# Reordering the prologue of a fused attention and two-layer MoE kernel: seven first-layer chunks of batch 1 moved into the first script

## The chip, the cores and the metric

The kernel runs on one core of one Trainium2 chip. The metric is the device time of one execution in microseconds (us). Three runs of the kernel before gave 869.15, 870.41 and 870.77 us; the median is 870.41 us.

## The reference

```python
# attention: 4 batches, 8 heads, 576 positions, head size 64
scores = (1/8) * q @ k.T          # heads 0-3: window of 32; heads 4-7: window of 128, every 4th
attn = softmax(where(mask, scores, -1e9))
x = attn @ v                      # -> 2304 tokens x 512
# first block, d_ff = 1536
h = sigmoid(x @ w_gate) * (x @ w_val)
y = h @ w_out                     # 2304 x 512
# second block, d_ff = 2048
h2 = y @ w_in
out = (max(h2,0) + alpha*min(h2,0)) @ w_out2
```

All inputs and outputs are float32. q, k and w_gate are scaled up, so that the softmax and the sigmoid are sharp.

## The kernel before

Every large product is made from float16 halves: an operand is scaled by a power of two, its high half is a float16 copy and its low half is what the copy leaves. Three matmuls (high x high, high x low, low x high) then stand for one float32 product. So each weight goes through a **preparation**: a load (SP queue), a decode of three bit operations for each 512-column piece (VectorE, `decode`, L180, L184, L188), a bound (ScalarE, `bound`, L195), a power of two from it (a one-column matmul at L149, two small VectorE operations in `root_power`, one on GpSimd), and a split into high and low half. `split_weight` does the split either with two ScalarE copies and a GpSimd subtraction (L169), or, with its `on_dve` flag, with one ScalarE copy and one VectorE operation (L173).

The work goes batch by batch. A half-batch `hb` is one batch and one kind of head (0, 1 are batch 0; 2, 3 batch 1; 4 belongs to batch 2). For each there are scores (`qk_mm`, `qk_sub`), softmax (`exponent`, `p_sums`, `p_scale`), a transpose, and the product with v (`pv_mm`, `pv_x`), which leaves x in halves in `xh`.

The first layer has 12 **chunks** of 128 gate and 128 value columns. Chunk m of batch b is `gv_mm(b, m, "g")` and `gv_mm(b, m, "v")` (24 matmuls each, L582, also callable by halves of 12), then `gv_sigmoid` (ScalarE), `gv_multiply` (VectorE, L600, frees the value's PSUM pair) and `gv_halves` (a ScalarE copy, and a subtraction on GpSimd or VectorE, L169), which leaves the tile `gt[b, m]`. The second product of the block, `o1_mm(b, d, ...)` (L627, `d` = 0 to 3, quarters of 18 matmuls in the first script), reads all twelve `gt` tiles of its batch and the split `w_o`. `o1_y` takes it out of PSUM and stores it to `y_dram`. Three pairs of PSUM banks rotate over all g, v and o products.

The order of the prologue is written out by hand: the string `FIRST` is a list of tasks, run one after the other, and every engine and the SP queue execute their instructions in that order. Some task names: `lqk hb`, `lv hb`, `lgv m`, `lo d r` are loads of q and k, v, gate and value weights of chunk m, and a third of output weights d; `dec`, `spl` are decode and split of chunk m; `odec`, `orow`, `ospl` the same for the output weights, `opow` their power of two; `g`, `v`, `sig`, `mul`, `half` the parts of a chunk; `o`, `oy` those of the second product; `plo`, `pm` the low half and the scaling of the softmax; `prep n` some steps of the preparation of the second block's weights; `warm n` n matmuls on zeros. A last argument of 1 or 0 on `spl`, `ospl`, `plo`, `half` chooses VectorE or GpSimd.

In the kernel before, `FIRST` holds all of batch 0's first layer, its `o` products with three chunks of batch 1 behind and between the last of them, and the attention of half-batches 0 to 3 and the scores and softmax of 4. After it come loops: for batch 1 the chunks from `EARLY` on, then its `o`, then batches 2 and 3; the last batch overlaps the second block. `prepare(n)` gives out steps of the second block's preparation at two places of every chunk and three of every `o` product. Loaded words and v tiles share a pool `yp` of 8 buffers of 4 KB for each partition; the `gt` tiles of a batch share 12 buffers of a pool `gp`.

```python
for m in range(EARLY if b == 1 else 0, M1):
    gv_mm(b, m, "g")
    if m:
        gv_halves(b, m - 1, late)
    gv_sigmoid(b, m)
    prepare(3)
    gv_mm(b, m, "v")
    gv_multiply(b, m)
```

Of the kernel before, what the change touches and what calls it, by code (L numbers as in the profile page):

```python
# [1567 lines left out]
wsum 0; phi 1 0; pvx 0 1 0; plo 1 0 0; plo 1 2 0; wpow 0; pvm 1 0; pvx 0 1 1; dec 1; pvm 1 1 4; spl 0 0; pvx 1 1 1;
spl 0 1; g 0 0 0; pvx 1 0 0; pvx 1 0 1; lgv 4; wb 1; wsum 1; qkm 2 0; wpow 1; pvx 1 1 0; spl 1 0; wgs 0; g 0 0 1; dec
2; g 0 1 0; wgs 1; spl 1 1 1; lgv 5; dec 3; wb 2; v 0 0 0; wsum 2 0; sig 0 0; qkm 2 1; lgv 7; wpow 2; spl 2 0 1; spl 2  # L1570
1 1; v 0 0 1; wb 3; g 0 1 1; wgs 2; mul 0 0; wsum 3; wpow 3; spl 3 0; v 0 1 0; sig 0 1; v 0 1 1; lo 1 0; g 0 2 0; spl
3 1; v 0 2 0; g 0 2 1; dec 4; mul 0 1; qks 2 0; xb 2; xb 3; wb 4; qkm 2 2; sig 0 2; lo 0 0; xsum 1; half 0 1 1; wsum
4; v 0 2 1; dec 5; g 0 3 0; qks 2 1; wpow 4; wb 5; wsum 5 0; g 0 3 1; qks 2 2; spl 4 0; spl 4 1 1; half 0 0 1; wpow 5;
mul 0 2; exp 2; v 0 3 0; dec 6; wgs 3; sig 0 3; v 0 3 1; xpow 1; spl 5 0 1; lgv 8; wb 6; spl 5 1 1; g 0 4 0; wsum 6; v
0 4 0; wgs 4; half 0 2 1; mul 0 3; lgv 10; wpow 6; spl 6 0; g 0 4 1; sig 0 4; spl 6 1; dec 7; wgs 5; g 0 5 0; wb 7;
half 0 3; v 0 4 1; wsum 7; rs 2; g 0 5 1; lgv 9; sig 0 5; wpow 7; g 0 6 0; mul 0 4; wgs 7; spl 7 0; pm 2; v 0 5 0; dec
8; v 0 5 1; tr 2; spl 7 1; g 0 6 1; wb 8; wgs 6; v 0 6 0; wsum 8; half 0 4; wpow 8; dec 9; sig 0 6; vhi 2; g 0 7 0;
mul 0 5; lv 4; phi 2; v 0 6 1; spl 8 0; lqk 3; g 0 7 1; plo 2; spl 8 1 1; wb 9; sig 0 7; lgv 11; mul 0 6; vlo 2; half
0 6 1; half 0 5 1; g 0 8 0; wsum 9 0; lo 0 2; v 0 7 0; lo 0 1; wpow 9; g 0 8 1; dec 10; pvm 2 0; pvx 2 0 1; spl 9 0;
spl 9 1 1; wgs 8; v 0 7 1; wb 10; wsum 10; mul 0 7; v 0 8 0; pvx 2 0 0; wpow 10; sig 0 8; dec 11; spl 10 0 1; spl 10  # L1580
1; v 0 8 1; g 0 9 0; half 0 7 1; wb 11; pvm 2 1; wsum 11; g 0 9 1; pvx 2 1 0; v 0 9 0; odec 0 0 1 2; wpow 11; wgs 9;
orow 0 0 0; v 0 9 1; lo 2 0; orow 0 1 1; pvx 2 1 1; spl 11 0; orow 0 2 0; lo 2 2; qkm 3 0; lo 1 1; qks 3 0; spl 11 1
1; qkm 3 1; mul 0 8; wgs 10; g 0 10 0; xb 4; vhi 3; obd 0 1; obd 0 0; odec 1 0 1; lo 3 1; osum 0; half 0 8 1; qkm 3 2;
sig 0 9; opow 0; v 0 10 0; g 0 10 1; mul 0 9; v 0 11 0; vlo 3; half 0 9 0; wgs 11; v 0 10 1; lo 1 2; odec 1 2; ospl 0
0 1; qks 3 2; qks 3 1; lo 2 1; orow 1 2 0; sig 0 10; lo 3 2; orow 1 0 1; mul 0 10; orow 1 1 0; v 0 11 1; g 0 11 0; g 0
11 1; ospl 0 1; obd 1 0; lqk 4; obd 1 1; osum 1; o 0 0 0; exp 3; odec 2 0 1 2; opow 1; sig 0 11; orow 2 2 0; orow 2 1
1; mul 0 11; orow 2 0 1; o 0 0 1; rs 3; ospl 1 0 1; half 0 11 1; obd 2 1; obd 2 0; pm 3; osum 2; ospl 1 1; o 0 0 2;
# [89 lines left out]
```

## Time and profile before

| what | value |
|---|---|
| runs, us | 869.15, 870.41, 870.77 (median 870.41) |
| span of the profiled execution, first to last instruction | 870.0 us |
| TensorE busy, mean granted clock | 830.0 us (95%), 0.982 of full speed |
| VectorE, ScalarE, GpSimd busy | 618.3, 440.7, 286.7 us |
| DMA | 166.9 MB, mean 192 GB/s |
| the chain that ended last, by engine | PE 76%, DVE 13%, ACT 5%, DMA 4% |
| last matmul of `FIRST` ends (720th of L582) | 206.4 us |
| from 206.4 to 400 us | TensorE busy 193.6 of 193.6 us |

The profile shows one execution; its own time is the span, and what lies around the span is not recorded. The median of the runs is 0.4 us above it. PE is TensorE's matmuls, DVE VectorE, ACT ScalarE, POOL GpSimd, SP the queue that issues all transfers. A busy engine runs an instruction; "<-" after an idle time names what ended it. A granted clock of 1.00 is the upper of TensorE's two levels, 2.4 GHz; a mean between 0.5 and 1 says for how much of a stretch the lower, 1.2 GHz, was granted.

### The profile page before, as it was taken

The numbers are of one execution on the slowest core, as the hardware profiler recorded it, in microseconds if no ns is written. First come the engines' busy times: TensorE is split into PE (matmuls) and PEld (weight loads), VectorE is DVE, ScalarE is ACT, GpSimd is POOL, SyncE is SP. The second block draws the span as 40 slices with busy tenths as digits, with TensorE's granted clock in tenths as the row PEclk, the third lists the DMA queues.
The fourth block names the chain that finished last, engine by engine and source line by source line (L and its number), as shares of the span: only waits on it lengthen the run. The fifth ranks groups of instructions, "written<-read, shape, count | busy, mean of one in ns | idle before, by whom it ended". The sixth has DMA issues, their size and how long they took to land.

```text
span 870.0 us, 21031 instructions
## 1 busy us (share of the span) xinstructions
PE 830.0 (95%) x8994; PEld 686.7 (79%) x8994; DVE 618.3 (71%) x1031; ACT 440.7 (51%) x730; POOL 286.7 (33%) x261
## 2 busy tenths in 40 slices
...
GB/s 323 286 194 124 229 100 207 15 173 102 92 95 169 139 136 119 50 68 264 301 166 223 342 214 221 337 241 218 308 203 212 243 210 194 225 309 194 122 230 73
DMA packets 85181, 166.91 MB, mean 192 GB/s; under 512 B 5344, under 2 KB 57696, under 8 KB 85088
## 3 DMA queue, kind: packets, MB, share of 16 engines
...
## 4 chain that ended last, share of the span: by engine, by line
PE 76%; DVE 13%; ACT 5%; DMA 4%; issue 2%; POOL 1%; SPq 0%; ACTq 0%; DVEq 0%
PE banks L582 27%; PE banks L1204 18%; PE banks L959 17%; PE banks L627 11%; DVE plain L188 2%; DVE plain L184 2%; DVE plain L180 2%; PE banks L430 1%; PE banks L316 1%; DMA words<-w_out 1%; DMA words<-w_gate 1%; ACT junk L195 1%; DVE plain L199 1%; DMA w_i<-wi_dram 1%; DVE g_g L1045 1%
## 5 line engine op out<-in xcount | busy, mean ns | idle before, releaser
L582 PE MATMUL banks<-xh,w_gv 128*128 128x288 f16 x2304 | 295.5, 290 | 3.1 <-DVE gf L600 2.3
L582 PEld LDWEIGHTS <-w_gv 128*128 128x128 f16 x2304 | 226.1, 99 | 63.3 <-issue 3.2
L959 PE MATMUL banks<-yh,w_i 128*128 128x256 f16 x1536 | 187.1, 273 | 5.1 <-DMA w_i<-wi_dram 1.6
L959 PEld LDWEIGHTS <-w_i 128*128 128x128 f16 x1536 | 150.0, 98 | 24.0 <-issue 3.3
L627 PE MATMUL banks<-gt,w_o 128*128 128x288 f16 x1152 | 147.0, 288 | 0.3 <-POOL gt L169 0.2
L627 PEld LDWEIGHTS <-w_o 128*128 128x128 f16 x1152 | 112.0, 98 | 29.4 <-issue 0.4
L1204 PEld LDWEIGHTS <-g_gv 128*128 128x128 f16 x780 | 76.3, 98 | 8.8
L1204 PE MATMUL banks<-w,g_gv 128*128 128x256 f16 x612 | 75.5, 273 | 0.0
L997 ACT ACTIVATE neg<-banks 128x512 f32<-128x512 f32 x72 | 42.8, 594 | 57.2 <-DVE banks L1017 40.8
L1055 POOL TENSOR_TENSOR yh<-temp_y 128x512 f32<-128x512 f32 x16 | 26.5, 1659 | 125.7 <-DVE temp_y L1005 121.0
L600 DVE SCALAR_TENSOR_TENSOR gf<-banks,sg 128x576 f32<-128x576 f32 x48 | 36.0, 751 | 38.9 <-PE banks L582 27.3
L165 POOL TENSOR_SCALAR sc<-sc 128x1 f32<-128x1 f32 x35 | 11.4, 326 | 157.7 <-DVE sc L161 157.7
L1204 PEld LDWEIGHTS <-g_g 128*128 128x128 f16 x564 | 55.2, 98 | 6.4
L169 POOL TENSOR_TENSOR gt<-gf,gt 128x576 f16<-128x576 f32 x24 | 36.8, 1533 | 63.5 <-ACT gt L610 63.3
L195 ACT ACTIVATE junk<-plain 128x1024 bf16<-128x1024 f32 (+1 forms) x36 | 36.2, 1006 | 40.3 <-DVE plain L199 28.3
L595 ACT ACTIVATE sg<-banks,sc 128x576 f32<-128x576 f32 x48 | 35.3, 735 | 38.1 <-PE banks L582 27.7
L610 ACT ACTIVATE gt<-gf 128x576 f16<-128x576 f32 x48 | 32.3, 676 | 41.3 <-DVE gf L600 41.3
L188 DVE SCALAR_TENSOR_TENSOR plain<-words,plain 128x512 uint32<-128x512 uint32 x68 | 50.8, 767 | 1.2
L184 DVE SCALAR_TENSOR_TENSOR plain<-words,plain 128x512 uint32<-128x512 uint32 x68 | 50.2, 759 | 1.2
L1204 PE MATMUL banks<-w,g_g 128*128 128x256 f16 x396 | 48.3, 273 | 0.0
L1005 DVE SCALAR_TENSOR_TENSOR temp_w<-neg,sc,banks 128x256 f32<-128x256 f32 x64 | 27.8, 475 | 25.1 <-ACT neg L997 25.1
L1045 DVE SCALAR_TENSOR_TENSOR g_gv<-temp_w,sc,g_gv 128x256 f16<-128x256 f32 (+1 forms) x37 | 26.0, 711 | 27.6 <-ACT g_gv L1041 27.6
...
## 6 DMA issues: line engine op xcount, KB each, us to landing
...
```

The costliest lines, as they stand in the source:

```text
L169: engine.tensor_tensor(out=lo, in0=src, in1=hi, op=ALU.subtract)
L184: nc.vector.scalar_tensor_tensor(out=d, in0=hi, scalar=0xC0000000, in1=d, op0=ALU.bitwise_and, op1=ALU.bitwise_or)
L188: nc.vector.scalar_tensor_tensor(out=d, in0=lo, scalar=29, in1=d, op0=ALU.logical_shift_right, op1=ALU.bitwise_or)
L195: nc.scalar.activation(junk[:, :src.shape[1]], src, AF.Square, accum_out=dst)
L582: nc.tensor.matmul(ps[:, h, :], lhsT=a, rhs=x_[:, H2 * h:H2 * h + H2], start=(kk == 0 and i == 0), stop=(kk == KD - 1 and i == 2),)
L595: nc.scalar.activation(halves(sg), ps, AF.Sigmoid, scale=sgx[b][:, m:m + 1])
L600: nc.vector.scalar_tensor_tensor(out=halves(gf), in0=ps, scalar=2.0 ** -15, in1=halves(sg), op0=ALU.mult, op1=ALU.mult)
L627: nc.tensor.matmul(ps[:, h, :], lhsT=a, rhs=x_[:, H2 * h:H2 * h + H2], start=(m == 0 and z == 0), stop=(m == M1 - 1 and z == 2),)
L959: nc.tensor.matmul(o, lhsT=h, rhs=l, start=(new and v == 0 and q == 1), stop=(q == total_), skip_group_check=True,)
L997: nc.scalar.activation(t[:, :2 * n], src[:, :2 * n], AF.Relu, scale=-1.0)
L1045: nc.vector.scalar_tensor_tensor(out=h[:, 1], in0=x_, scalar=s_al, in1=h[:, 0], op0=ALU.mult, op1=ALU.subtract)
L1204: nc.tensor.matmul(ps[:, H4 * t:H4 * t + H4].rearrange("p (c f) -> p c f", c=2), lhsT=a, rhs=x_, start=(first and k == 0 and t == 0 and z ...
```

## The change

`EARLY` goes from 3 to 7, so seven chunks of batch 1 (0 to 6) are tasks of `FIRST`, and the loop of batch 1 begins with chunk 7. Their order there is 1, 0, 2, 4, 5, 3, 6, and all stand ahead of batch 0's first `o`. Their `gt` tiles cannot all stay on chip while batch 0's twelve are in use: a new tag holds two (`HELD`), and tiles 1, 0, 4, 3 and 2 are stored to a DRAM tensor `g_dram` (`gst`) and loaded back into `gp` (`gld`) after batch 0's last `o`. Tiles 5 and 6 stay. The third piece of each output weight is decoded into a buffer of its own (`po`) and no longer into one of `yp`, and the `y` tile of `o1_y` shares the buffers of the sigmoid in place of those of `gf`.

```diff
-    EARLY = 3
+    EARLY = 7
+    HELD = 2
...
-            plain["o", d, 1] = yp.tile([P, 4, P], F32, tag="y", name="plain")
+            plain["o", d, 1] = wp.tile([P, 4, P], F32, tag="po", name="po")
...
+    g_dram = dp.tile([EARLY - HELD, P, 2, S], F16, name="g_dram")
...
-        if b == 1 and m < EARLY - 1:
-            t = gt[b, m] = ap.tile([P, 2, S], F16, tag=f"g{m}", name="gt")
+        if b == 1 and m < EARLY:
+            t = gt[b, m] = ap.tile([P, 2, S], F16, tag="g", name="gt", bufs=HELD)
...
+    def g_store(m):
+        nc.sync.dma_start(out=g_dram[m], in_=gt.pop((1, m)))
+
+    def g_load(m):
+        t = gt[1, m] = gp.tile([P, 2, S], F16, tag="g", name="gt")
+        nc.sync.dma_start(out=t, in_=g_dram[m])
...
-        dst = tp.tile([P, S], F32, tag="gf", name="y")
+        dst = tp.tile([P, S], F32, tag="sg", name="y")
...
-        "wgs": lambda m: x_gate_scale(0, m, m + 1),
+        "wgs": lambda m, b=0, e=0: x_gate_scale(b, m, max(e, m + 1)),
...
-        "gs": lambda b: x_gate_scale(b, 0, M1),
...
-            for m in range(EARLY if b == 1 else 0, M1):
+            m0 = EARLY if b == 1 else 0
+            for m in range(m0, M1):
                 gv_mm(b, m, "g")
-                if m:
+                if m > m0:
                     gv_halves(b, m - 1, late)
...
 FIRST = """
-lqk 0 3; warm 6 2; warm 8 5; lqk 1 3; qkm 0 0; qks 0 0; qkm 0 1; exp 0 0; qks 0 1 1; qkm 0 2; lv 0; exp 0 1; lv 1; rs
+lgv 0; dec 0 0; dec 0 1; lqk 0 3; warm 6 2; wb 0; warm 8 5; qkm 0 0; qkm 0 1; wsum 0; qks 0 0; wpow 0; lqk 1 3; exp 0
...
```

The whole of `FIRST` is written in a new order. Counted over it, 31 more instructions run on VectorE (322 for 291) and 7 fewer on GpSimd (81 for 88): on VectorE are now 12 of the `half` subtractions (2 before), 16 of the weight splits (10), 5 of the `plo` (none), 4 of the `ospl` (5), 19 of the `mul` (15) and 20 instructions of `prep` (13). On GpSimd stand 6 fewer `spl`, 5 fewer `half` and 5 fewer `plo`, one more `ospl`, and small one-column operations. The matmuls on zeros are the same 28, and the loads of activation tables are the same 14 in the whole program.

The head of the SP queue, which issues all transfers (words are weight pieces, second is q and k of half-batch 1, vc is v). Before:

```order
L1303 DMA mask_sb_80<-mask 128x516
L246 DMA k_93<-kt 128x2x224
L247 DMA q_92<-qbd 128x2x384
L246 DMA second_117<-kt 128x2x224
L252 DMA vc_173<-vk 128x1152
L252 DMA vc_181<-vk 128x1152
L499 DMA words_213<-w_gate 128x4x256
L499 DMA words_215<-w_val 128x4x256
```

And now:

```order
L1313 DMA mask_sb_80<-mask 128x516
L500 DMA words_93<-w_gate 128x4x256
L500 DMA words_95<-w_val 128x4x256
L247 DMA k_105<-kt 128x2x224
L248 DMA q_104<-qbd 128x2x384
L247 DMA second_169<-kt 128x2x224
L500 DMA words_279<-w_gate 128x4x256
L500 DMA words_281<-w_val 128x4x256
L253 DMA vc_283<-vk 128x1152
```

The rows between that repeat these kinds are left out: q and k come in three pairs for each half-batch. The weights of chunk 0 moved from behind all of half-batches 0 and 1 to the very front, and those of chunk 1 ahead of v.

VectorE between the last split of the first layer's weights (w_gv) and the first decode of the output weights (words to plain). Now:

```order
L174 SCALAR_TENSOR_TENSOR w_gv_1590<-plain,sc,w_gv_1590 128x4x128
L400 STREAM_TRANSPOSE pt<-s 128x1152
L276 SCALAR_TENSOR_TENSOR vh<-vc,sc,vh 128x1152
L170 TENSOR_TENSOR s<-pt,s 128x1152
L170 TENSOR_TENSOR gt<-gf,gt 128x576
L602 SCALAR_TENSOR_TENSOR gf<-banks,sg 128x576
L174 SCALAR_TENSOR_TENSOR xh<-banks,xh 128x2x144 x2
L181 TENSOR_SCALAR plain<-words 128x512 x2
```

Rows that repeat an earlier kind are left out. In the kernel before, the first decode of output weights (9 instructions) stood ahead of chunk 11's last split, and half-batch 3's v came 17 rows behind that decode and its transpose 46 rows. They now come first, so that batch 1's x is complete before any output weight is decoded. The two rows at L170 are a `plo` and a `half` that GpSimd did before.

The SP queue where the five tiles are stored and loaded back. Now:

```order
L616 DMA g_dram_85<-gt_2366 128x1152
L533 DMA words_2570<-w_out 128x4x256
L533 DMA words_2574<-w_out 128x4x256
L247 DMA k_2626<-kt 128x2x608
L248 DMA q_2625<-qbd 128x2x1152
L616 DMA g_dram_85<-gt_2526 128x1152
L616 DMA g_dram_85<-gt_2682 128x1152
L533 DMA words_2801<-w_out 128x4x256
L616 DMA g_dram_85<-gt_2798 128x1152
L616 DMA g_dram_85<-gt_2596 128x1152
L620 DMA gt_3170<-g_dram_85 128x1152
```

Nothing of this was there before. The first store is that of tile 1; the second and third, of tiles 0 and 4, stand behind two loads of output weights and the load of q and k of half-batch 5, which waits for the last scores of half-batch 4. Between the last store and the first load back stand loads of the second block's weights and of v, and three `y` stores (left out).

## Rows read from the trace of the kernel before

**Rows 1.** Stretches: us, PE, PEld, DVE, ACT, POOL busy (instructions), clock, DMA share, GB/s.
```profile
0.00:40.00 40.00, 29.64 (x606) 20.50 (x608) 27.22 (x61) 22.38 (x65) 12.65 (x19) 0.87 0.97 331
40.00:122.40 82.40, 71.48 (x833) 54.50 (x829) 71.20 (x127) 54.38 (x86) 43.85 (x43) 0.92 0.49 160
122.40:169.20 46.80, 38.42 (x406) 28.93 (x403) 41.71 (x59) 26.80 (x43) 24.95 (x23) 0.93 0.36 123
169.20:206.40 37.20, 37.18 (x471) 29.94 (x471) 25.80 (x44) 20.10 (x29) 7.12 (x9) 1.00 0.43 148
0.00:206.40 206.40, 176.72 (x2306) 133.87 (x2307) 165.92 (x290) 123.66 (x220) 88.57 (x93) 0.93 0.54 182
...
400.00:600.00 200.00, 195.28 (x1903) 162.29 (x1902) 153.76 (x236) 108.08 (x187) 88.97 (x81) 1.00 0.70 245
600.00:870.00 270.00, 264.42 (x2420) 236.29 (x2417) 162.82 (x279) 124.66 (x205) 89.57 (x70) 1.00 0.59 216
```

**Rows 2.** The chain that ended last, in order of time: start us, us, what.
```profile
119.74 6.30 DMA words<-w_out
```

**Rows 3.** The same chain where TensorE runs without waiting.
```profile
179.81 4.52 PE banks L627 x36
...
244.01 5.99 PE banks L582 x48
```

**Rows 4.** Waits of VectorE from 0 to 124 us: us in total, times, longest.
```profile
DVE mx L347 <- PE banks L316: 7.7, 1, 7.7
DVE xh L173 <- ACT xh L172: 5.7, 3, 2.9
DVE pt L399 <- POOL s L381: 3.1, 1, 3.1
```

**Rows 5.** Timeline: decodes of chunk 5 and chunk 10, and GpSimd beside the second.
```profile
57.63 0.75 DVE L180 TENSOR_SCALAR plain<-words 128x512 uint32<-128x512 uint32 x2
...
59.51 1.28 DVE L188 SCALAR_TENSOR_TENSOR plain<-words,plain 128x512 uint32<-128x512 uint32 x2
...
97.59 3.81 POOL L169 TENSOR_TENSOR gt<-gf,gt 128x576 f16<-128x576 f32 x2
...
99.03 2.66 DVE L180 TENSOR_SCALAR plain<-words 128x512 uint32<-128x512 uint32 x2
...
103.77 1.28 DVE L188 SCALAR_TENSOR_TENSOR plain<-words,plain 128x512 uint32<-128x512 uint32 x2
```

**Rows 6.** Groups of VectorE instructions, 0 to 124 us: busy us, mean ns.
```profile
L188 DVE SCALAR_TENSOR_TENSOR plain<-words,plain 128x512 uint32<-128x512 uint32 x27 | 20.8, 809 | 0.1
L184 DVE SCALAR_TENSOR_TENSOR plain<-words,plain 128x512 uint32<-128x512 uint32 x27 | 20.2, 787 | 0.1
L180 DVE TENSOR_SCALAR plain<-words 128x512 uint32<-128x512 uint32 x27 | 13.9, 554 | 0.5 <-DMA words<-w_gate 0.4
L173 DVE SCALAR_TENSOR_TENSOR w_gv<-plain,sc,w_gv 128x512 f16<-128x512 f32 x10 | 9.8, 993 | 2.9 <-ACT w_gv L172 2.7
L600 DVE SCALAR_TENSOR_TENSOR gf<-banks,sg 128x576 f32<-128x576 f32 x8 | 6.0, 748 | 0.0
```

**Rows 7.** Groups of GpSimd instructions, 0 to 124 us: busy us, mean ns.
```profile
L169 POOL TENSOR_TENSOR w_gv<-plain,w_gv 128x512 f16<-128x512 f32 x14 | 19.1, 1364 | 16.2 <-ACT w_gv L206 16.2
L169 POOL TENSOR_TENSOR gt<-gf,gt 128x576 f16<-128x576 f32 x8 | 12.6, 1582 | 6.5 <-ACT gt L610 6.4
...
L169 POOL TENSOR_TENSOR s<-pt,s 128x1152 f16<-128x1152 f32 x1 | 2.8, 2822 | 0.0
```

**Rows 8.** The same form of subtraction on VectorE, 0 to 206.4 us.
```profile
L169 DVE TENSOR_TENSOR gt<-gf,gt 128x576 f16<-128x576 f32 x2 | 3.3, 1639 | 1.0 <-ACT gt L610 1.0
```

**Rows 9.** Issues of the first 45 us: KB each, median us to landing.
```profile
k<-kt SPq DMA_DIRECT2D x1, 224.0 KB, 2.9
```

**Rows 10.** Transfers to and from y_dram, from issue to landing.
```profile
DMA to landing us min/median/max: 2.1/3.8/12.7
```

**Rows 11.** Waits of the SP queue from 0 to 210 us: us in total, times, longest.
```profile
SPq L499 <- DVE plain L188: 44.6, 9, 9.5
```

More of the change, by code (lines that the diff above doesn't have):

```diff
@@ L1288, in attention_moe_kernel @@
         "half": gv_halves,
+        "gst": g_store,
+        "gld": g_load,
         "o": o1_mm,
         "oy": o1_y,
-        "gs": lambda b: x_gate_scale(b, 0, M1),
         "alpha": alpha_scale,
@@ L1568 @@
[L1568 to L1587, printed above, removed]
@@ L1593 @@
-phi 4; mul 1 0; g 1 1 0; g 1 1 1; v 1 1 0; g 1 2 0; half 1 0 0; sig 1 1; v 1 1 1; g 1 2 1; plo 4; prep 6; v 1 2 0; mul
-1 1; prep 6; lv 6; sig 1 2; v 1 2 1; mul 1 2; half 1 1
+lgv 0; dec 0 0; dec 0 1; lqk 0 3; warm 6 2; wb 0; warm 8 5; qkm 0 0; qkm 0 1; wsum 0; qks 0 0; wpow 0; lqk 1 3; exp 0
+0; qkm 0 2; qks 0 1 1; exp 0 1; qks 0 2 1; rs 0 0; pm 0 0 0; qkm 1 0 4; qks 1 0; exp 1 0; rs 0 1; exp 0 2; qkm 1 1 5;
+rs 1 0; tr 0 0; pm 0 1 0; qkm 1 2 0; qks 1 2 1; pm 1 0 0; qks 1 1; exp 1 2; lgv 1; lv 0; tr 1 0; phi 1 0; exp 1 1; dec
@@ new lines @@
+1; rs 1 2; warm 14 3; lv 1; xb 0; rs 0 2; rs 1 1; pm 1 2 0; xb 1; tr 0 1; xsum 0 0; pm 1 1 0; xpow 0; lgv 2; tr 1 2;
+tr 1 1; plo 1 0 1; pm 0 2 0; spl 0 0 1; lv 3; pv32 0 0 6; tr 0 2; wb 1; wsum 1; lal; pvx 0 0 1; phi 1 1; phi 1 2; pvx
+0 0 0; pv32 0 1 4; lv 2; plo 1 1 0; plo 1 2 1; lgv 3; vhi 1; spl 0 1 0; vlo 1; pvm 1 0; wpow 1; pvx 0 1 0; pvx 0 1 1;
+pvm 1 1 4; dec 2; pvx 1 0 1; pvx 1 0 0; spl 1 0 0; lqk 2; g 0 0 0; pvx 1 1 0; wgs 0; g 0 1 0; lgv 4; spl 1 1 1; pvx 1
+1 1; wb 2; xb 3; dec 3; qkm 2 0; g 0 0 1; wsum 2 0; wgs 1; wpow 2; g 0 1 1; qks 2 0; qkm 2 1; wgs 2; sig 0 0; v 0 1 0;
@@ new lines @@
+qks 2 1; qkm 2 2; wb 3; spl 2 0 1; wsum 3; wpow 3; spl 2 1 0; v 0 0 0; v 0 1 1; lgv 6; v 0 0 1; qks 2 2; spl 3 0 1;
+dec 4; sig 0 1; exp 2; spl 3 1 0; mul 0 1; wgs 3; g 0 2 0; half 0 1 1; mul 0 0; wb 4; v 0 2 0; xb 2; rs 2; g 0 2 1;
+wsum 4; dec 6; lgv 5; xsum 1; xpow 1; pm 2; half 0 0 0; sig 0 2; v 0 2 1; lqk 3; g 0 3 0; wpow 4; mul 0 2; spl 4 0 1;
+tr 2; g 0 3 1; v 0 3 0; v 0 3 1; lo 2 0; spl 4 1 0; lgv 10; wb 6; dec 5; vhi 2; sig 0 3; g 0 4 0; mul 0 3; vlo 2; phi
+2; g 0 4 1; v 0 4 0; wb 5; lgv 8; wsum 5 0; wgs 4; wpow 5; wsum 6; v 0 4 1; plo 2 0 1; wpow 6; half 0 3 0; spl 5 0 1;
@@ new lines @@
+spl 5 1 0; sig 0 4; mul 0 4; pvm 2 0; wgs 5; pvx 2 0 1; lgv 7; g 0 5 0; pvx 2 0 0; v 0 5 0; lo 1 1; v 0 5 1; spl 6 0
+1; spl 6 1 1; g 0 5 1; sig 0 5; pvm 2 1; dec 7; dec 8; g 0 6 0; lgv 9; half 0 4 0; wb 7; pvx 2 1 0; half 0 2 1; g 0 6
+1; wsum 7; wpow 7; lo 0 2; wb 8; wgs 6; wsum 8; wgs 7; qkm 3 0; v 0 6 0; mul 0 5; wpow 8; pvx 2 1 1; spl 7 0 1; spl 7
+1 1; qkm 3 1; v 0 6 1; spl 8 0 1; spl 8 1 1; g 0 7 0; g 0 7 1; lgv 11; sig 0 6; dec 9; dec 10; lv 5; v 0 7 0; wb 9;
+wsum 9 0; mul 0 6; sig 0 7; half 0 5 1; wpow 9; spl 9 0 1; v 0 7 1; mul 0 7; g 0 8 0; wgs 8; g 0 8 1; lv 6; qks 3 0; v
@@ new lines @@
+0 8 0; spl 9 1 0; dec 11; lo 0 1; qks 3 1; wb 10; v 0 8 1; g 0 9 0; wsum 10; wpow 10; sig 0 8; vhi 3; half 0 6 1; wb
+11; lo 3 2; wgs 10; qkm 3 2; qks 3 2; wsum 11; v 0 9 0; spl 10 0 1; wgs 9; exp 3; mul 0 8; wgs 2 1; wpow 11; wgs 1 1;
+rs 3; half 0 8 1; v 0 9 1; spl 11 0 1; g 0 9 1; lo 1 0; g 0 10 0; g 0 10 1; sig 0 9; sig 0 10; g 0 11 0; mul 0 9; pm
+3; g 0 11 1; spl 11 1 1; tr 3; wgs 11; v 0 11 0; spl 10 1 0; v 0 11 1; vlo 3; phi 3; plo 3 0 1; v 0 10 0; half 0 7 0;
+pvm 3 0; sig 0 11; v 0 10 1; mul 0 11; g 1 1 0; pvx 3 0 0; wgs 4 1; pvx 3 0 1; wgs 0 1; half 0 11 0; pvm 3 1; g 1 0 0;
```

22 lines of the change are left out of this document (13 added, 9 removed).

## The prediction

> **What bounds the kernel now.** I read the stretches first [rows 1]. Behind 206.4 us, where the hand-written script ends, TensorE waits little: 4.7 us in 400 to 600 and 5.6 us in 600 to 870, and nothing in 206.4 to 400. In front of it, 176.7 of 206.4 us are busy, so 29.7 us are idle, and the granted clock is 0.93, which for 176.7 busy us is another 12 us. Nearly all of this lies before 169.2 us. So about 42 us are lost in the prologue. The reader is to see who is busy there instead: VectorE, 71.2 of 82.4 us between 40 and 122.4 and 41.7 of 46.8 behind it. A chunk of the first layer costs TensorE 6.0 us [rows 3], and VectorE brings its weights more slowly than that.
>
> VectorE's own losses before 122.4 us are 24.0 us (82.4 + 40.0 - 71.2 - 27.2). The waits name the largest [rows 4]: 7.7 us for the first scores, 5.7 us for x, 3.1 us for a scaling on GpSimd. The chain of waits adds a load of output weights that is late by up to 6.3 us [rows 2].
>
> VectorE is also slowed. Six decode instructions of chunk 5 last from 57.63 to 60.79, 3.16 us; the six of chunk 10, with GpSimd at work beside them, from 99.03 to 105.05, 6.02 us [rows 5]. Over the stretch 81 decode instructions take 54.9 us [rows 6]; at chunk 5's pace they would take 42.7, so 12.2 us are lost, and I put 5 us on the splits (0.99 us each, against some 0.75 unhindered), the long subtraction and x. GpSimd's tile operations there sum to about 47 us, the largest groups of them in [rows 7]. So one us of GpSimd costs VectorE about 17.5/47 = 0.37 us.
>
> **TensorE's work.** At full clock the script before is 176.7 x 0.93 = 164.3 us. The change moves four more chunks into it, 4 x 5.99 = 24.0 us [rows 3], which are taken out of the loop behind; no matmul is added or dropped. So the new script is 188.3 us of full-speed work, and the point to compare with is 206.4 + 24.0 = 230.4 us. What the change can gain is idle time and low clock inside the script.
>
> **VectorE up to the last chunk of batch 0.** Chunk 11's first matmuls wait for its first split on VectorE. Before, the matching split starts at 122.4, behind 98.4 us of work and 24.0 of waiting. Ahead of it the new order adds five splits (5 x 0.74), three `half` (3 x 0.75, taken as the product of the same width [rows 6], since no unhindered one is shown; the other bound is 1.64 [rows 8]), three `plo` (2.5 in all, by width), two score blocks (2.2), the softmax sums of half-batch 3 (1.8) and one product (0.75): 13.2 us. It takes away the first output decode (9 x 0.68) and one scaling (0.7): 6.8 us. GpSimd gives up seven splits (7 x 1.36), three `half` (3 x 1.58), three `plo` (5.1 in all) and two scalings (2.5), 21.8 us [rows 7], which at 0.37 returns 8.1 us. VectorE's work is 98.4 + 13.2 - 6.8 - 8.1 = 96.7 us.
>
> Its waits: chunk 0's weights are now first in the queue. Of the start's 7.7 us I keep 6.8: a first load lands 2.9 us after its issue at 1.2 us when it has 224 KB [rows 9], the weights have twice that for each half, so decoding starts near 4.8, ends near 8.5, and q and k, behind 1 MB at some 360 GB/s, come 2.9 us later than before. The 3.1 us for GpSimd go, since five instructions now stand between that scaling and the transpose. Of the 5.7 us for x I keep half. That makes 24.0 - 0.9 - 3.1 - 2.9 = 17 us. Bounds: 8 us, if only the start is left, and 26, as before and 2 for the later q and k.
>
> So chunk 11 is ready at 96.7 + 17 = 114 us. TensorE's program has 21 half-chunk products ahead of it, 504 matmuls, 62.9 us at 5.99 for 48 [rows 3], and nearly all of what is neither chunk nor `o` in the script: 164.3 less 15 chunks (89.9) and 16 quarters (288 at 4.52 for 36, 36.2) is 38.2, less about 5 for half-batch 4's scores and half-batch 3's PV, 33. That is 96 us. TensorE has then lost 114 - 96 = **18 us**. The earlier chunks give no more by the same count.
>
> **Behind that point** VectorE has the output weights to do, and TensorE 92 us of work in hand, 41.9 us of it batch 1's chunks, which need no new weights: batch 1's x now stands ahead of the output decode. Before, TensorE had next to nothing there and lost 8.4 us of 46.8 at clock 0.93. Not all is hidden: an output decode of nine instructions (some 5 us) can stand ahead of a product that frees PSUM, and the two-tile ring waits on stores. I take 4 us; bounds 0 and 10.
>
> The script then ends at 188.3 + 18 + 4 = 210.3, against 230.4: a gain of 20 us.
>
> **Costed at nothing.** The five stores and loads (288 KB each) cover themselves: the loads back are first read after five more chunks, 30 us, against 12.7 us for the slowest y transfer [rows 10]; uncovered they would cost that once. The late output load [rows 2] goes, since the new buffer leaves the pool to the loads and each now has over 14 us of VectorE work between the release of its buffer and its reader; what is late next is the decode itself. The `y` tile in the sigmoid's buffers waits at most for its own store, off TensorE's path; a store's landing if not. The second block's preparation loses some calls in batch 1's loop and gets three more in the script, so it comes a few steps later, under TensorE's work; its price is a rival below.
>
> The sum is made against the span, 870.0; the median of the runs is 0.4 above. 870.0 - 20.1 + 0.4 gives **850 us**.
>
> **Rivals.**
> *A, the forecast*: 850, its own range 840 to 858 (waits of VectorE 8 to 24).
> *B, VectorE stays the bound through the output weights.* VectorE's work in the whole script is 165.9 + 22.1 for 31 instructions - 9.1 for 24.7 us that leave GpSimd = 179; about 12 of it is behind the last output scale. With 20 us of waits that scale is ready at 187, and its split, behind a softmax scaling on GpSimd, at 192; TensorE reaches the last `o` at 210 - 9 = 201. Nine us of slack. If GpSimd's slowing doesn't fall (+9) and VectorE waits as now (+9), it is ready at 210 and the end moves by 9: 859. For it speaks that what moves to VectorE is hindered there too, 1.64 us [rows 8]; against it, that GpSimd's work falls. The Trainium skill (GPSIMD Engine Reference, Key points) says that GpSimd shares its SBUF interfaces with VectorE and contends with instructions in a 2-port perf mode or with two SBUF inputs. By that, the moved subtractions and splits are all of the hindered kind, and and at 1.64 for 0.75 on the eleven moved ones ahead of chunk 11, a third of the time beside GpSimd, the sum would be some 3 us later; the trace agrees with it for the product from PSUM, at 0.748 without spread [rows 6], and goes beyond it, since the decode's one-input step is stretched most [rows 5].
> *C, given back behind the script.* Batch 1's loop is shorter by 24 us with nearly the same preparation in the program; if the waits behind 400 us (10.3) double, 860.
> *D, slower: the two-tile ring.* Stores 0 and 4 stand in SP's queue behind q and k of half-batch 5, which wait for scores, and behind output weights, which wait for decodes; SP waits up to 9.5 us at once now [rows 11]. A tile's round is a ScalarE copy and a subtraction (2.2 us), the wait in the queue and 3.8 to 12.7 us to landing [rows 10]. Two tiles serve two chunks, 12 us; a round of 20 us for seven tiles is 3.5 x 20 = 70 us where the chunks take 42, and ScalarE stands still meanwhile: 28 us on 850, 878. It decides from a round over 12 us. Against it: `half` 1, 0, 2 need no second store, and chunks are spread over 46 us of program.
> *E, no change*: TensorE's idle only moves, because later scores cost what earlier weights give; 870.
>
> **Chances.** A 0.62, B 0.16, C 0.07, D 0.07, E 0.05; 0.03 for something better than A's range. Anything under 0.2% (1.7 us) can't be told from no change. Faster: A, C, the better cases and nearly all of B, 0.87; same: E, 0.05; slower: D and a rest, 0.08. The range 838 to 865 takes A with both ends of VectorE's waits (gain 32 to 6, the second with 10 us behind chunk 11), B and C.
>
> **What would show it.** First decode near 5 us and first chunk matmul near 34, as before; chunk 11's first matmuls near 115; TensorE without gaps from there at clock 1.00; the last matmul of the script near 210; decodes nearer 3.2 than 4 us a chunk. B would show VectorE over 90% busy and TensorE idle ahead of the last `o`; C idle time between 300 and 600; D ScalarE's copy waiting for a store. I am wrong if chunk 11 starts later than 125 or the gap behind it is over 10 us.

## The result, and the profile after

The changed kernel takes 857.41 us (856.0 to 859.5, four runs) where the kernel before, beside it on the same chip, takes 870.59: a ratio of 0.9855, 95% interval 0.9832 to 0.9878. The forecast was 850 with a range of 838 to 865. The profiled run has a span of 856.1 us.

Line numbers are those of the changed kernel: decoding is L181, L185, L189 (L180, L184, L188 before), splits on VectorE L174, the chunks' matmuls L584, the outputs' L636, the second block's first layer L968.

The stretches, as in [rows 1] (us, then PE, PEld, DVE, ACT, POOL busy with instructions, clock, DMA share, GB/s), now cut where the prediction cuts them: at 113.17, when chunk 11's first split starts on VectorE, and at 207.75, when the script's last matmul ends.

```profile
0.00:40.00 40.00, 29.01 (x577) 21.33 (x578) 28.23 (x69) 22.35 (x65) 10.13 (x19) 0.78 1.00 344
40.00:113.17 73.17, 71.32 (x891) 55.75 (x890) 64.96 (x129) 52.21 (x80) 23.29 (x33) 0.98 0.53 172
113.17:207.75 94.58, 93.38 (x1036) 74.55 (x1034) 67.44 (x119) 50.32 (x77) 32.34 (x32) 1.00 0.40 134
207.75:476.00 268.25, 267.08 (x3202) 212.88 (x3200) 202.21 (x321) 125.73 (x185) 57.25 (x47) 1.00 0.50 169
476.00:494.10 18.10, 13.07 (x105) 9.95 (x103) 11.93 (x16) 10.22 (x18) 10.98 (x9) 0.99 0.81 268
489.20:500.00 10.80, 6.67 (x43) 4.87 (x43) 4.95 (x8) 5.96 (x12) 6.71 (x10) 0.84 0.84 275
```

From 40 us to the script's end TensorE idles 3.05 us (1.85 and 1.20). Its large losses are now ahead of 40 us and, new, between 476 and 500. VectorE's waits ahead of chunk 11 (us in total, times, longest), as in [rows 4]:

```profile
DVE plain L181 <- DMA words<-w_gate: 5.6, 1, 5.6
DVE sc L158 <- PE banks L150: 3.5, 3, 1.9
DVE mx L348 <- PE banks L317: 3.3, 3, 1.5
DVE xh L174 <- ACT xh L173: 2.4, 3, 1.6
```

The wait for GpSimd's scaling, 3.1 us before, is gone. VectorE's groups of the same stretch (busy us, mean ns), as in [rows 6]:

```profile
L185 DVE SCALAR_TENSOR_TENSOR plain<-words,plain 128x512 uint32<-128x512 uint32 x24 | 15.5, 684 | 0.1
L189 DVE SCALAR_TENSOR_TENSOR plain<-words,plain 128x512 uint32<-128x512 uint32 x24 | 15.5, 683 | 0.1
L174 DVE SCALAR_TENSOR_TENSOR w_gv<-plain,sc,w_gv 128x512 f16<-128x512 f32 x15 | 11.0, 754 | 1.0 <-ACT w_gv L173 0.8
L181 DVE TENSOR_SCALAR plain<-words 128x512 uint32<-128x512 uint32 x24 | 9.1, 417 | 6.1 <-DMA words<-w_gate 5.6 <-POOL w_gv L170 0.5
...
L170 DVE TENSOR_TENSOR gt<-gf,gt 128x576 f16<-128x576 f32 x3 | 2.2, 749 | 0.0
```

The first decoding step falls from 554 ns to 417, the other two from 809 and 787 to 684, a split from 993 to 754.

**Where the gain went.** The same matmul can be found in both traces by counting those of its form from the start. How much earlier it ends in the changed kernel is called the lead here:

```
matmul                                      before    after    lead
batch 1's last chunk (1152nd L584)           263.7    241.6    22.1
batch 1's last output (576th L636)           302.3    281.0    21.3
batch 3's last chunk (2304th L584)           491.5    469.8    21.7
last output ahead of L968 (1014th L636)      509.9    489.2    20.7
batch 3's last output (1152nd L636)          547.8    533.2    14.6
last matmul of the first layer (1536th L968) 828.1    814.3    13.7
```

So the script gained 22.1 us, two more than forecast, and 8.4 us were given back, 6.1 of them at one place: between the last output ahead of the second block's first matmuls and the outputs behind them. The timeline there (start us, us, engine line op, then the idle time ahead of it and what ended it):

```profile
487.68 0.72 ACT L823 ACTIVATE halves<-plain,sc 128x512 f16<-128x512 f32 x1 [0.32 <-DVE halves L828]
489.11 0.74 DVE L828 SCALAR_TENSOR_TENSOR halves<-quarter,sc,halves 128x512 f16<-128x512 f32 x1
490.36 0.71 ACT L823 ACTIVATE halves<-plain,sc 128x512 f16<-128x512 f32 x1
490.97 0.71 ACT L925 ACTIVATE yh<-y,sc 128x512 f16<-128x512 f32 x1
491.72 0.27 PE L968 MATMUL banks<-yh,w_i 128*128 128x256 f16 x1 [2.54 <-ACT yh L925]
492.56 0.49 PE L968 MATMUL banks<-yh,w_i 128*128 128x256 f16 x3 [0.57 <-DVE yh L929]
494.09 2.29 PE L968 MATMUL banks<-yh,w_i 128*128 128x256 f16 x10 [1.04 <-DVE yh L929]
```

TensorE waits for the second block's input `yh`, and ScalarE and VectorE still write `halves` ahead of it: the last step of preparing the output weights of the second block. Between 489.2 and 500 TensorE works 6.67 of 10.8 us at clock 0.84. In the kernel before, the same matmuls take 4.7 us without a gap, and the last `yh` is ready at 505.4 (504.88 + 0.47), 4.4 us before TensorE's first matmul of that layer at 509.75 (`yh` by VectorE is L920 there, the matmuls are L959):

```profile
504.88 0.47 DVE L920 SCALAR_TENSOR_TENSOR yh<-ys,sc,yh 128x256 f16<-128x256 f32 x1
509.75 1.47 PE L959 MATMUL banks<-yh,w_i 128*128 128x256 f16 x12
509.90:514.60 4.70, 4.70 (x44) 3.99 (x42) 0.87 (x2) 1.43 (x4) 3.77 (x6) 1.00 0.18 66
```

The last store of prepared weights is issued at 501.6 us before and at 494.7 now, which is 515.4 with the lead of 20.7 added that the last output ahead of it has. Against TensorE's work the preparation ends 14 us later.

### The profile page after: what moved, and what is told of

Same layout as the page of the kernel before. It is cut to its first block, busy times and chain, and to the rows that moved or that the text cites. A ratio compares the mean times of both kernels' runs of the same rounds, so it can differ in the third digit from the quotient of the medians.

```text
span 856.1 us, 21080 instructions
## 1 busy us (share of the span) xinstructions
PE 826.2 (97%) x8994; PEld 686.5 (80%) x8994; DVE 601.8 (70%) x1046; ACT 438.4 (51%) x725; POOL 263.8 (31%) x253
## 4 chain that ended last, share of the span: by engine, by line
PE 72%; DVE 12%; DMA 9%; ACT 3%; issue 2%; SPq 2%; POOL 0%; ACTq 0%; DVEq 0%
PE banks L584 20%; PE banks L1213 18%; PE banks L968 17%; PE banks L636 13%; DMA w_dram<-halves 2%; DVE plain L189 2%; DMA plain_dram<-plain 2%; DVE plain L185 2%; PE banks L317 2%; PE banks L431 1%; DVE halves L828 1%; DMA vc<-vk 1%; DMA q<-qbd 1%; DVE plain L181 1%; DVE gf L602 1%
## 5 line engine op out<-in xcount | busy, mean ns | idle before, releaser
L584 PE MATMUL banks<-xh,w_gv 128*128 128x288 f16 x2304 | 290.6, 287 | 0.5 <-ACT sg L597 0.3
L584 PEld LDWEIGHTS <-w_gv 128*128 128x128 f16 x2304 | 223.3, 98 | 58.4 <-issue 0.9
L968 PE MATMUL banks<-yh,w_i 128*128 128x256 f16 x1536 | 189.1, 274 | 10.0 <-ACT yh L925 2.5
L968 PEld LDWEIGHTS <-w_i 128*128 128x128 f16 x1536 | 150.6, 98 | 30.3 <-issue 8.0
L636 PE MATMUL banks<-gt,w_o 128*128 128x288 f16 x1152 | 144.5, 286 | 0.9 <-POOL gt L170 0.9
L636 PEld LDWEIGHTS <-w_o 128*128 128x128 f16 x1152 | 111.8, 98 | 28.9 <-issue 1.1
L196 ACT ACTIVATE junk<-plain 128x1024 bf16<-128x1024 f32 x32 | 33.8, 1057 | 36.0 <-DVE plain L200 18.8
L170 POOL TENSOR_TENSOR gt<-gf,gt 128x576 f16<-128x576 f32 x19 | 27.7, 1457 | 75.4 <-ACT gt L612 75.2
L189 DVE SCALAR_TENSOR_TENSOR plain<-words,plain 128x512 uint32<-128x512 uint32 x64 | 47.7, 765 | 1.2
L1023 ACT ACTIVATE temp_y<-banks 128x512 f32<-128x512 f32 x32 | 19.0, 595 | 50.9 <-PE banks L968 50.7
L185 DVE SCALAR_TENSOR_TENSOR plain<-words,plain 128x512 uint32<-128x512 uint32 x64 | 43.8, 704 | 1.2
```

Source lines behind the costliest of these rows:

```text
L170: engine.tensor_tensor(out=lo, in0=src, in1=hi, op=ALU.subtract)
L185: nc.vector.scalar_tensor_tensor(out=d, in0=hi, scalar=0xC0000000, in1=d, op0=ALU.bitwise_and, op1=ALU.bitwise_or)
L189: nc.vector.scalar_tensor_tensor(out=d, in0=lo, scalar=29, in1=d, op0=ALU.logical_shift_right, op1=ALU.bitwise_or)
L196: nc.scalar.activation(junk[:, :src.shape[1]], src, AF.Square, accum_out=dst)
L584: nc.tensor.matmul(ps[:, h, :], lhsT=a, rhs=x_[:, H2 * h:H2 * h + H2], start=(kk == 0 and i == 0), stop=(kk == KD - 1 and i == 2),)
L636: nc.tensor.matmul(ps[:, h, :], lhsT=a, rhs=x_[:, H2 * h:H2 * h + H2], start=(m == 0 and z == 0), stop=(m == M1 - 1 and z == 2),)
```

## Experiments

The first question was why the gain shrinks behind 476 us. Theory 1: a step of the preparation is issued when calls of `prepare` have given it columns; batch 1's loop lost eight calls (four chunks, two each) and the script gained three, so every later step moved to a later place in the program. By the rules of `prepare` (at most six columns saved up, some steps three calls apart) I placed every step: from batch 1's second product on, the changed kernel has each step two to five calls later, most of them three or four. (Where the expectation below says five chunks, it is these four.)

**p1, the places put back.**

```
-                prepare(3)
+                prepare(6 if b == 1 else 3)
                 gv_mm(b, m, "v")
```

> One number: in batch 1's loop the first call of prepare in a chunk gives 6 columns in place of 3, so that from batch 2 on each step of the second block's preparation stands at the chunk or output slice where it stood before the change. Theory 1 (the gain of the script, 21.7 us at the last product of batch 3's chunks, was given back because five chunks' calls of prepare are gone and the preparation ends 14 us later against TensorE's work): the waits ahead of the first second-block matmuls (about 5 us between 478 and 494, and the clock of 0.96 there) go, the lead stays near 21 us to the end, 850 us. Rival 2 (the DMA queues are full there, share 0.91 between 460 and 500, and the same transfers in a shorter time wait wherever they are put): the lead still falls to about 15, 856 to 858. Rival 3 (VectorE has no room in batch 1's loop, the waits only move there): TensorE idle 4 to 7 us between 210 and 290, 856 to 858.

Measured: 850.08 us, ratio to before 0.9766 (0.9752 to 0.9781). The lead is 21.8 at batch 1's last output and 21.2 from 479 us to the end. The stretch from 460 to 500 has 39.54 us of TensorE at full clock (34.97 at 0.96 in the changed kernel), and of its waits between 468 and 490 one is left:

```profile
460.00:500.00 40.00, 39.54 (x331) 32.13 (x330) 26.09 (x28) 20.16 (x35) 26.58 (x25) 1.00 0.78 260
```

```profile
PE banks L636 <- POOL gt L170: 0.5, 1, 0.5
```

Theory 1 holds. Rival 2 falls: the script is as short as in the changed kernel and its transfers as close together, and the lead does not fall to 15; in this stretch the DMA share is 0.78 in place of 0.91. Rival 3 falls: between 200 and 300 us TensorE idles 0.03 us.

**b1, the other way round: the kernel before, with its preparation made late.**

```
-half 1 0 0; sig 1 1; v 1 1 1; g 1 2 1; plo 4; prep 6; v 1 2 0; mul 1 1; prep 6; lv 6;
+half 1 0 0; sig 1 1; v 1 1 1; g 1 2 1; plo 4; prep 6; v 1 2 0; mul 1 1; lv 6;
```

> The kernel BEFORE the change without the last call of prepare in its script: from the middle of batch 1's second layer on each step of the preparation stands where the changed kernel has it, and nothing else is changed. Theory 1: the same loss without any of the change's gain, about 7 us between 490 and 512, 877 to 878 us. Rival 2 (it takes the shorter script, with its transfers closer together, to lose time): no change, 870 to 871.

Measured: 879.03 us, ratio 1.0102 (1.0078 to 1.0127). The lead is -0.3 us at batch 1's last chunk, -1.4 at batch 3's last chunk, -2.4 at the last output ahead of the second block and -8.7 behind its first matmuls. TensorE's waits from 500 to 520, and the stretch around them (L959 and L627 are here what L968 and L636 are in the changed kernel):

```profile
PE banks L959 <- ACT yh L916: 2.2, 1, 2.2
PE banks L627 <- POOL gt L169: 0.9, 1, 0.9
PE banks L959 <- DVE yh L920: 0.8, 2, 0.6
```

```profile
512.20:523.40 11.20, 8.14 (x45) 5.47 (x44) 4.70 (x8) 5.73 (x12) 7.58 (x10) 0.70 0.81 266
```

The same waits for the same tiles, without anything else of the change: the loss at this place comes from the preparation's place alone. The stretch is 6.5 us longer than in the kernel before (11.2 for 4.7): 3.1 of that is idle, and the same matmuls are busy 8.1 us in place of 4.7, at a clock of 0.70.

**p2, the preparation earlier than ever.**

```
-prepare(3 - (0 if late else ATTENTION.get(m, 0)), sums=False)
+prepare(3 - (0 if late else ATTENTION.get(m, 0) - 2), sums=False)
```

> The second call of prepare in each chunk of batches 1 and 2 gives two columns more: the preparation is up to a call earlier than in the kernel before, at its end by one call. Theory 1: 850 us, as with the other edit, since TensorE waits for the preparation no more and has nothing further to win from it. Rival 2 (queues full): 856 to 858. Rival 3 (VectorE has no room, and this edit asks for more in the chunks with attention work): worse than the other edit by 2 us or more.

Measured: 854.78 us, ratio 0.9824 (0.981 to 0.9838). The wait behind 476 is gone (the lead stays 16.3 from there on), but the lead falls from 21.7 to 16.3 between 325 and 400 us, 4.5 of it between 388 and 397, where the timeline shows what went ahead of batch 3's `xh`:

```profile
389.01 0.69 DVE L200 TENSOR_TENSOR plain<-plain,sc 128x512 f32<-128x512 f32 x1
389.62 1.43 DVE L174 SCALAR_TENSOR_TENSOR xh<-banks,xh 128x288 f16<-128x288 f32 x2
390.47 0.18 PE L431 MATMUL banks<-s,vh 32*64 32x32 f16 x1 [2.55 <-DVE xh L174]
```

VectorE decodes the second block's output weights (L181 to L200) in front of the splits that free TensorE's PSUM banks; the clock between 380 and 400 is 0.83. This is rival 3, for this edit: the preparation has a window. Ending 14 us late costs 7 us, and this earlier placing costs 5.

The second question was what in the script earned the 22 us.

**e2, batch 1's chunks put behind the output slices**, in the changed kernel (preparation late, as there). All `g`, `v`, `sig`, `mul` and `half` of batch 1 go behind `oy 0 3`; `gst` and `gld` fall away:

```
-        if b == 1 and m < EARLY:
-            t = gt[b, m] = ap.tile([P, 2, S], F16, tag="g", name="gt", bufs=HELD)
-        else:
-            t = gt[b, m] = gp.tile([P, 2, S], F16, tag="g", name="gt")
+        t = gt[b, m] = gp.tile([P, 2, S], F16, tag="g", name="gt")
```

> The changed kernel with all products, sigmoids and splits of batch 1's seven chunks taken out of their places and put behind batch 0's last output slice, without the five stores and loads; all else in the changed order. Theory 1 (the 42 us of chunks that need no new weights cover the output weights' way through VectorE): TensorE is idle 20 to 40 us between 125 and 200, chunk 11 starts near 115 as now, and the lead at the script's end falls from 22 us to under 8; 864 to 880 us. Rival 4 (the gain comes from the new order and the engines of batch 0's part alone, TensorE would have lost little behind it): the lead at the script's end stays over 15 us, 858 to 864.

Measured: 895.66 us, ratio 1.0295 (1.0276 to 1.0314). At batch 1's last output TensorE is 15.7 us behind the kernel before.

```profile
115.00:140.00 25.00, 11.44 (x308) 9.23 (x308) 19.95 (x30) 8.64 (x13) 4.78 (x5) 0.80 0.37 135
140.00:170.00 30.00, 13.57 (x127) 10.27 (x124) 20.23 (x43) 13.59 (x23) 9.93 (x15) 0.61 0.50 167
```

```profile
PE banks L317 <- DMA q<-qbd: 12.9, 1, 12.9
PE banks L150 <- ACT junk L196: 9.6, 3, 7.4
PE banks L150 <- DVE sc L846: 6.5, 1, 6.5
```

TensorE idles 30 us between 115 and 170 (55 - 25.0), as Theory 1 said, and the 25 us that it works run at 0.80 and 0.61. The size was missed: the clock takes some 8 us more, and one wait of 12.9 us for q of half-batch 4 comes from the edit itself, which takes away the work that stood in front of that load's reader. The other 17 us are waits behind the output weights: 9.6 for the bounds of these weights and 6.5 for a sum that stands behind their decoding in VectorE's program. Without the chunks the changed order is worse here than the kernel before. Rival 4 falls even if the wait for q and the whole loss of clock are forgiven, since the lead would then be some 5 us (-15.7 + 12.9 + 8) and not over 15; how much the order alone would cost with that load placed well was not tried.

The runs from here on are edits of p1, so 850.1 us and a script's lead of 21.8 us are what they compare with.

**e3, work back to GpSimd** (one task for each kind here):

```
-... plo 1 0 1; ... spl 0 0 1; ... half 0 4 0; ... spl 2 1 0; ...
+... plo 1 0 0; ... spl 0 0; ... half 0 4; ... spl 2 1 1; ...
```

> On the version with the preparation put back (850.1 us): ten splits, six `half` and three `plo` that the change gave to VectorE go back to GpSimd, four splits that it gave to GpSimd go back to VectorE; the order is the changed one. Theory 1 (the prediction's rate, one us of GpSimd costs VectorE 0.37): ahead of chunk 11 GpSimd gets some 16 us, VectorE loses some 8 us of its own and 6 us come back as slowing, so VectorE's work is about the same; lead at the script's end 21 to 24 us, 848 to 851 us. Rival 5 (the slowing costs more than the rate says, or the longer way of a split through ScalarE and GpSimd, 2.7 us in place of 1.4, makes weights late): lead 3 us or more lower, 853 to 858 us.

Measured: 856.14 us, ratio 0.9839 (0.982 to 0.9859); lead 15.4. Up to the 288th chunk matmul (84 us) it is level with p1 within 0.5 us; at the 336th it is 6.3 us behind, and it stays so. VectorE's decodes of chunks 7 and 8 there:

```profile
81.16 1.80 DVE L181 TENSOR_SCALAR plain<-words 128x512 uint32<-128x512 uint32 x2
82.89 1.28 DVE L185 SCALAR_TENSOR_TENSOR plain<-words,plain 128x512 uint32<-128x512 uint32 x2
...
85.29 1.84 DVE L181 TENSOR_SCALAR plain<-words 128x512 uint32<-128x512 uint32 x2
87.05 2.36 DVE L185 SCALAR_TENSOR_TENSOR plain<-words,plain 128x512 uint32<-128x512 uint32 x2
89.33 1.28 DVE L189 SCALAR_TENSOR_TENSOR plain<-words,plain 128x512 uint32<-128x512 uint32 x2
```

And in the changed kernel (p1 has the same lines 0.07 us later):

```profile
80.69 0.76 DVE L181 TENSOR_SCALAR plain<-words 128x512 uint32<-128x512 uint32 x2
...
83.77 0.75 DVE L181 TENSOR_SCALAR plain<-words 128x512 uint32<-128x512 uint32 x2
84.44 1.29 DVE L185 SCALAR_TENSOR_TENSOR plain<-words,plain 128x512 uint32<-128x512 uint32 x2
85.65 1.29 DVE L189 SCALAR_TENSOR_TENSOR plain<-words,plain 128x512 uint32<-128x512 uint32 x2
```

The twelve instructions end at 90.6 in place of 86.9. The three lines that are longer lie beside GpSimd's subtractions (80.2 to 82.7, 85.6 to 86.9, 87.5 to 88.9), each by 1.04 to 1.09 us for 1.3 to 1.5 us side by side; the others are as in the changed kernel. TensorE, which adds up a chunk's bounds ahead of its next scores, waits 3.7 us for that; in p1 the same wait is 0.5 us:

```profile
PE banks L150 <- ACT junk L196: 4.2, 2, 3.7
```

A clock of 0.89 between 70 and 100 (1.00 in p1) goes with it. Rival 5 holds: a rate evenly spread per us of GpSimd forecasts little here, since nearly all of the cost falls where the two engines meet on the path. The run also shows that VectorE has next to nothing to spare near 88 us: what its decodes lose there, TensorE waits.

**e4, chunk 0's weights second.**

```
-lgv 0; dec 0 0; dec 0 1; lqk 0 3; warm 6 2; wb 0; warm 8 5; qkm 0 0; qkm 0 1; wsum 0; qks 0 0; wpow 0; lqk 1 3;
+lqk 0 3; warm 6 2; warm 8 5; lgv 0; qkm 0 0; qkm 0 1; qks 0 0; dec 0 0; dec 0 1; wb 0; wsum 0; wpow 0; lqk 1 3;
```

> On the same version: the load of chunk 0's weights goes back behind q and k of half-batch 0, and its decoding and power behind the first block of scores on VectorE. Theory 1 (VectorE is the bound up to chunk 11, and what it does while it waits for scores is won): TensorE's first scores come some 2 us earlier (near 7), the first decode some 4 us later, chunk 11's start moves from 113 to 114 to 116, lead 18 to 21 us, 850 to 853 us. Rival 6 (weights first cost TensorE's start, first chunk matmul at 39 in place of 34.6, clock 0.65 between 20 and 40): first chunk matmul near 36, lead 23 us or more, 847 to 849 us.

Measured: 855.02 us, ratio 0.983 (0.9807 to 0.9852); lead 16.9. VectorE waits for the scores first and for the weights then:

```profile
8.47 0.56 DVE L348 TENSOR_REDUCE mx<-banks 128x6 f32<-128x384 f32 x1 [8.47 <-PE banks L317]
9.06 0.56 DVE L349 TENSOR_TENSOR s<-banks,mx 128x384 f32<-128x384 f32 x1
11.60 0.43 DVE L181 TENSOR_SCALAR plain<-words 128x512 uint32<-128x512 uint32 x1 [1.98 <-DMA words<-w_gate]
```

Decoding starts at 11.6 in place of 5.7, and the first chunk's matmuls come 5.0 us later. Theory 1 had the sign and was short by half, and Rival 6 falls. What nobody expected is that the shift is rigid: 5.2 us at the 24th chunk matmul, 5.2 at the 576th, 4.9 at the script's end.

**e7 and e8, the start once more.** From that came a new theory, that TensorE itself is the bound from its first chunk on.

```
-pvm 1 1 4; dec 2; pvx 1 0 1; pvx 1 0 0; spl 1 0 0;
+pvm 1 1 4; pvx 1 0 1; pvx 1 0 0; dec 2; spl 1 0 0;
```

> On the version with the preparation put back (850.1 us, first chunk matmul at 39.8): chunk 2's decoding moves on VectorE behind the two splits of half-batch 1's first product, which TensorE's next PV waits for (VectorE does them at 37.5, behind the decoding of 34.4 to 37.5; TensorE idle 3.2 us until 38.3). Theory 9 (from the first chunk matmul on TensorE has no lasting wait, so that every us at the start arrives at the end, as the 5.2 us of the run with the weights second did): first chunk matmul near 37, lead of the script near 24 to 25, 847 to 848 us. Rival 10 (the prediction's count: VectorE sets chunk 11 at 114, and what TensorE wins before is lost until there): first chunk matmul near 37, but chunk 11 at the same time as before and lead within 1 us of 21.8, 849.5 to 850.5.

Measured: 849.88 us, ratio 0.9754 (0.9741 to 0.9767). TensorE's stop ahead of that PV shrank from 3.2 us to 2.5 only, so what ends it is not VectorE's decoding. What does is still open; the profile names no releaser. The first chunk came 0.4 us earlier, and so did every 48th chunk matmul up to the 576th.

e8 adds:

```
-exp 1 2; lgv 1; lv 0; ... lv 1;
+exp 1 2; lv 0; lv 1; lgv 1;
```

> The edit of the run before, and the two loads of v for batch 0 go ahead of chunk 1's weights in SP's queue (they land at 22.3 and 23.9, and TensorE waits 2.3 and 1.4 us for what ScalarE makes of them). Theory 9: another 1 to 2.5 us, first chunk matmul near 35, lead 25 to 27, 845 to 847 us, if chunk 1's weights, then some 2.9 us later, are still there for VectorE. Rival 10: lead still within 1 us of 21.8. Rival 11 (v's loads win nothing, since all transfers share queues that are full until 40 us, and chunk 1's weights become late): lead below that of the run before, 848 to 851 us.

Measured: 851.2 us, ratio 0.9777 (0.9761 to 0.9793). Chunk matmuls come 1.5 us later than in p1 from the 24th to the 576th. Rival 11 holds: the lead is below that of e7, and the time is 0.2 us above its range. Between 10 and 32 us the queues move 370 GB/s with all engines busy in e7 (365 in e8), and a load of v takes 9.9 us to land there:

```profile
vc<-vk SPq DMA_DIRECT2D x4, 576.0 KB, 9.9
```

Neither edit gained what was expected of it at the start. The shifts of -0.4, +1.5 and +5.2 us at the first chunk all arrive at the 576th unchanged, as Theory 9 said. They don't rule out Rival 10: e7's lead is within 1 us of 21.8, as that rival said, and in e4 and e8 VectorE's weights came later too. The trace of the changed kernel says more on this, in the next section.

**e5 and e6, two edits of the change undone.**

```
-            plain["o", d, 1] = wp.tile([P, 4, P], F32, tag="po", name="po")
+            plain["o", d, 1] = yp.tile([P, 4, P], F32, tag="y", name="plain")
```

> On the same version: the output decode's second buffer goes back from its own place into the pool that the loads use. Theory 1 (in the new order each load has over 14 us of VectorE work ahead of its reader, so the buffer was worth nothing here): lead within 1 us of 21.8, 849 to 851 us. Rival 7 (the buffer is what took the late output load off the path, up to 6.3 us before): a load of output weights on the chain again, lead 3 us or more lower, 853 us or more.

```
-        dst = tp.tile([P, S], F32, tag="sg", name="y")
+        dst = tp.tile([P, S], F32, tag="gf", name="y")
```

> On the same version: the tile y of the first layer's output goes back from the sigmoid's buffers to the product's. Theory 1 (costed at nothing): lead within 1 us, 849 to 851 us. Rival 8 (with batch 1's products next to batch 0's outputs, a product's buffer that waits for the store of y, 2 to 13 us to landing, holds TensorE): gaps of TensorE behind the first output slices, 852 to 858 us.

Measured: 849.27 us (ratio 0.9759, 0.974 to 0.9777) and 849.43 us (0.9777, 0.9742 to 0.9811); leads 22.2 and 22.4. Theory 1 holds in both; for e6 less surely, since one of its four runs took 854.9 us, the others 849.3 to 849.6, and the trace is of one of the others. In the new order neither buffer shows a worth in the medians or the traces.

## Why the prediction was right, and where it was not

The time lay inside the range and the sign was right. The script gained two us more than forecast. Behind it 8.4 us were given back, where the forecast had nothing, and 7.5 of these have one cause.

- **TensorE's work**, 188.3 us: 29.0 busy us at 0.78, 71.3 at 0.98 and 93.4 at 1.00 are 22.6 + 69.9 + 93.4 = 185.9. Held within 3 us.
- **VectorE up to chunk 11**: 96.7 us of work and 17 of waits were forecast, 114; measured are 93.2 and 20.0, 113.2. What GpSimd's lighter work returns was undersized, at 8.1 us. (The prediction's 17.5 should read 17.2, 12.2 + 5; the rate stays 0.37.) Counting 72 decoding instructions at chunk 5's pace gives 37.9 us and they take 40.1, so 2.2 us are lost where 12.2 were; with GpSimd's work 23.1 us smaller (33.4 against 12.65 + 43.85), that is 0.43 us per us from the decodes alone, and the splits come on top. Run e3 shows why a rate is a poor tool: the cost depends on what meets what. By the rule of the Trainium skill that stood beside this step (GPSIMD Engine Reference, Key points: GpSimd contends with VectorE's instructions of two SBUF inputs), the moved subtractions would have been hindered and the sum 3 us later; the three moved `half` took 749 ns each, no slower than the product. The prediction also said that the trace goes beyond the rule, because the one-input step is stretched most. That was a misreading: two of that step take 0.75 us where two of the others, on the same number of elements, take 1.28 [rows 5], so it runs at nearly twice their pace, as in a perf mode, which the rule names; no run here names the mode.
- **First chunk matmul "near 34, as before"**: at 39.0. This was wrong, and why is not shown. The weights of chunks 0 and 1, now ahead of v, push it back by 6 us (it lands at 22.3 and 23.8 us, at 16.1 and 17.6 before), and TensorE's product with it starts at 25.2 in place of 16.2. But with q and k of half-batch 0 ahead of the weights (e4) or v ahead of chunk 1's (e8) the first chunk came later still, at 44.7 and 40.6. The sum didn't use this time, because it let VectorE alone set chunk 11.
- **"The earlier chunks give no more"** failed: chunk 11 is not where TensorE waits for VectorE. Its first split is done at 113.8 us (113.17 + 0.65), and TensorE reaches the matmul that reads it, the 505th of L584, at 115.5, without a gap behind the one before. TensorE works 71.3 of 73.2 us between 40 and 113.17, so it is the bound from its first chunk on. VectorE is close behind: it has 1.7 us to spare at chunk 11 and next to nothing near 88 us (run e3), so that a start earlier by more would have met VectorE. TensorE has lost 113.2 - 92.5 = 20.7 us at that point, where 18 were forecast, but 17.4 of these are idle time and low clock ahead of 40 us (40.0 - 22.6). That the number held within 3 us, by a count of VectorE's work and waits that did not set it, is in part luck.
- **Behind that point**, 4 us within 0 and 10: 1.2 us. The cover of the seven chunks is real: e2 without it idles 30 us, 17 of them apart from the wait that the edit itself makes.
- **End of the script**: 210.3 forecast, 207.75 measured; gain 20.1 forecast, 22.1 measured.
- **Costed at nothing**: the buffers for `po` and `y` are confirmed by e5 and, with the doubt of one run, by e6. The stores and the two-tile ring cost TensorE no wait up to the script's end (rival D). Rival B's idle time ahead of the last output didn't come either.
- **The failed step** is the sentence that the preparation "comes a few steps later, under TensorE's work", and with it the 0.07 for rival C. It came 14 us later, where its last reader had 4.4 us to spare, and that cost 7.5 of the 8.4 us (the lead at the end is 21.2 in p1 and 13.7 here): 6.1 us at the second block's first matmuls, the rest in pieces of one us or less ahead of it and behind it. p1 too falls from 22.0 to 21.2, and that rest stays unexplained. Rival C had the mechanism, and 10 us for its price. p1 and b1 show the cause from both sides. A count of the calls by the rule of `prepare`, which stands in the program, would have shown the delay without a run, though not its price.

With that one step mended, p1 takes 850.1 us, 0.9% less than the changed kernel (0.9766 of the kernel before, against 0.9855). It is the best version here, together with e5, e6 and e7, which can't be told from it.
